# Block-sparse attention and an expert layer: V gathered in 2 KB rows on two queues, weight transfers behind the first V table, the first pairs normalised by VectorE

## The chip, the core and the metric

The kernel runs on one core of a Trainium2 chip. A core has five engines, each with its own in-order instruction queue: TensorE (PE, matmuls and transposes), VectorE (DVE), ScalarE (ACT), GpSimd (POOL) and SyncE (SP, which only issues transfers here). Sixteen DMA engines are shared by the transfers that SP, ACT and POOL issue. Matmuls write to PSUM, eight banks of 2 KB for each of 128 partitions; everything else lives in SBUF or in DRAM. The metric is the device time of one execution in microseconds.

## What is computed

Attention with 4 batches, 8 heads, 768 positions and 64 values per head, on a block mask: positions form 24 blocks of 32, and a query block sees its neighbours, the first and the last block, and three sampled blocks. The first and the last query block see everything. An expert layer with a swish follows.

```
scores = scale * np.matmul(q, k.transpose(0, 1, 3, 2))
mask = np.abs(blk_i - blk_j) <= window
mask = mask | (blk_i == 0) | (blk_j == 0) | (blk_i == n_blocks - 1) | (blk_j == n_blocks - 1)
# sampled_blocks: three more key blocks for each query block
scores = np.where(mask, scores, -1000000000.0)
attn = softmax(scores);  attn_out = np.matmul(attn, v)
x = attn_out.transpose(0, 2, 1, 3).reshape(B * S, H * D)      # 3072 x 512
h = x @ w_in                                                  # 512 x 2048
out = (h * (1.0 / (1.0 + np.exp(-beta * h)))) @ w_out         # 2048 x 512
```

All inputs are float32 (the sampled blocks are integers), and so is the output. Inside, the kernel works in float16 with float32 sums.

## The kernel before

**Attention in pairs.** Query blocks 1 to 22 of each batch form 11 pairs, 44 in all. For a pair n, POOL copies the three sampled key blocks of each of its two query blocks into a tile KG (`kg`, L521, block numbers read into registers), POOL or VectorE copies the neighbours and the first and last block (`kn`), TensorE adds the mask (L600) and the scores (`sc`, L610) into two PSUM banks. VectorE takes the maximum (L621), ScalarE the Exp (L629), VectorE the reciprocal of the sums (L635). The normalising multiply (`nrm`, L641) goes to POOL or VectorE, whichever the plan finds sooner. TensorE transposes the result (`tp`, L653), VectorE copies it out of PSUM (`ptv`, L657), TensorE multiplies it by the gathered V (`av`, L668), and VectorE and ScalarE copy the product into xT (L259, L257).

**V's way.** V is rearranged into Vn (`vperm`, L259 for batch 0), written to a DRAM table VT of 768 rows of 512 float16 values, 1 KB a row (`vtab`: L490 for batch 0 in two halves of the columns, L494 later), and gathered from there into VG, a tile of 128 partitions x 2 query blocks x 2 chunks x 512 values. For each pair SP issues seven transfers (L582): one with the neighbours of both blocks (96 partitions, 192 KB) and six with a sampled block each (32 partitions, 32 KB). The first pair of a batch has two more, with the first and the last block; the next three pairs copy that part from it (`vres`). Four VG tiles take turns. SP first reads a pair's six block numbers into registers (L550).

**The first and the last block** of a batch (`gs`, `gm`, `ge`, `gn`, `gt`, `gav`: L705 to L758) see all keys: four units per batch, each of which holds two banks for its scores.

**The expert layer** works on 96 blocks of 32 tokens in groups of 8, 8, 8, 16, 16, 16, 16 and 8. For a group, TensorE computes 16 row blocks of h (L817, four matmuls each), ScalarE the tanh (L823), VectorE the product g (L828); then TensorE multiplies by w_out (L845), ScalarE scales the result (L263) and issues the output transfer (L863). A group needs the attention output of all its blocks; the first one needs pairs 0 to 3.

**Loads.** SP loads K, Q and V of batch 0 in halves (L388, 768 KB each). POOL loads the weights with a cast to float16, eight transfers for each of w_in and w_out (L417, L423; 64 partitions, 256 KB of float16 each), after a small copy (L403) that waits for V's first half, and after them V, K and Q of batch 1 to 3 (L443).

**The order.** A list scheduler (`Plan.run`) writes the order of all engines once, when the kernel is built. Each task has an engine (or two to choose from), an assumed duration, predecessors, a priority, and PSUM banks to open or close. The scheduler steps through time and gives each free engine the ready task of lowest priority value. `prio` of pair n is 10 n. The transfers are modelled with one shared ring time, and weight transfers wait until the ring is at most 3.2 us ahead (`bulk`). The expert layer may hold four of the eight banks while attention is left. The engines then run that order, and wait with semaphores for what is really late.

Of the kernel before, what the change touches and what calls it, by code (L numbers as in the profile page):

```python
# [22 lines left out]
class Task:  # L23
    def __init__(self, name, eng, dur, emit, deps=(), prio=0.0, lat=0.0,
                 opens=(), closes=(), moe=False, dma=0.0, slack=0.0, hw=0, bulk=None):
        self.on = {eng: dur} if isinstance(eng, str) else dict(eng)
        self.name, self.eng, self.dur, self.emit = name, None, None, emit
        self.deps = [d for d in deps if d is not None]
        self.prio, self.lat = prio, lat
        self.opens, self.closes, self.moe, self.dma = opens, closes, moe, dma  # L30
        self.slack, self.hw, self.bulk = slack, hw, bulk
        self.kind = name.rstrip("0123456789.")
        self.end = None


class Plan:
# [14 lines left out]
    def run(self):  # L51
# [3 lines left out]
        need = {}  # L55
        for t in tasks:
            need[t] = len(t.deps)
# [10 lines left out]
        ring_at = 1.0  # L68
        lanes = [0.0] * 8
# [18 lines left out]
        while done < len(tasks):  # L88
            progress = False
            for e in engines:  # L90
# [3 lines left out]
                for t in waiting[e]:  # L94
# [7 lines left out]
                    if t.bulk is not None and ring_at > now + t.bulk + 1e-9:  # L102
                        continue
# [26 lines left out]
                if t.hw:  # L130
                    at = now
                    for _ in range(t.hw):
                        at = max(at, lanes[issued % 8]) + t.dur / t.hw
                        ring_at = max(ring_at, at + 0.4) + t.dma / t.hw
                        end = lanes[issued % 8] = ring_at + 0.9
                        issued += 1
                    free[e] = at
                elif t.dma:
                    ring_at = max(ring_at, end + 0.6) + t.dma
                    end = ring_at + 1.1  # L140
                t.start, t.end = now, end
                order.append(t)
                heapq.heappush(events, (end, seq, t))
                seq += 1
# [8 lines left out]
            for e in engines:  # L153
                nxt += [ready_at[t] for t in waiting[e] if ready_at[t] > now + 1e-9]
                nxt += [ring_at - t.bulk for t in waiting[e]
                        if t.bulk is not None and ring_at - t.bulk > now + 1e-9]
            nxt += [f for f, _ in bank_free if f > now + 1e-9]
            if not nxt:
                raise RuntimeError("plan is stuck: " + ", ".join(
                    t.name for e in engines for t in waiting[e]))  # L160
            now = max(now, min(nxt))
            while events and events[0][0] <= now + 1e-9:
# [3 lines left out]
                done += 1  # L166
                for s in succ.get(t, ()):
# [15 lines left out]
def kernel(  # L183
# [52 lines left out]
    VG = [sb(f"VG{i}", [P, 2, 2, D_MODEL]) for i in range(NVG)]  # L236
# [13 lines left out]
    plan = Plan(8, 4)  # L250
# [39 lines left out]
    t_sbl = add("sbl", "ACT", 0.5, emit_sbl, prio=-200, dma=0.3, hw=1)  # L290
# [46 lines left out]
    for part, f in enumerate((emit_mask0, emit_mask1, emit_mask2)):  # L337
# [9 lines left out]
    beta_row = osb[0][0:4, :]  # L347
    ident32 = t_sb[1][0:4, 0:8].bitcast(FP32)
    FQ = N_FFC // 4
    t_beta0 = add("beta", "ACT", 0.5, lambda: nc.scalar.dma_start(  # L350
        out=beta_row, in_=moe_beta.rearrange("(q x) -> q x", q=FQ)), prio=-140, dma=0.1, hw=1)
    t_id32 = add("id32", "DVE", 0.2, lambda: nc.vector.tensor_copy(
        out=ident32, in_=identity[0:4, 0:4]), deps=[t_ident], prio=-64)

    def emit_betaT():
        for i in range(4):
            nc.tensor.transpose(out=bank("beta")[:, i * FQ:(i + 1) * FQ],
                                in_=beta_row.rearrange("q (p i) -> q i p", i=4)[:, i, :], identity=ident32)
# [3 lines left out]
        out=beta_sb[:, :].rearrange("x (q i) -> x i q", i=4),  # L362
        in0=bank("beta")[:, 0:N_FFC].rearrange("x (i q) -> x i q", i=4),
# [22 lines left out]
    for i, (nm, t, dst) in enumerate((("K", k, K16), ("Q", q, Q16), ("V", v, None))):  # L386
        for f in range(2):
            tl = add(f"ld{nm}0.{f}", "SP", 0.47, lambda i=i, t=t, f=f: nc.sync.dma_start(  # L388
                out=stage_half(i, f) if i < 2 else v_stage[:, f * HH:(f + 1) * HH, :],
                in_=src6(t, 0, f * HH, HH)), prio=-80 + i * 2 + f, dma=2.0, hw=1)  # L390
# [11 lines left out]
    def touch(dst, src, dep, prio):  # L402
        return add("touch", "POOL", 0.6, lambda: nc.gpsimd.tensor_copy(out=dst, in_=src),  # L403
                   deps=[dep], prio=prio)

    tch = touch(w_in_sb[0:1, 0, 0:1], v_stage[0:1, 0, 0:1], v0ld[0], -58)


    w_in_r = moe_w_in.rearrange("(c p) f -> c p f", p=P)
    w_out_r = moe_w_out.rearrange("(q p i) m -> q p (i m)", p=P, i=4)  # L410
    w_in_v = w_in_sb[:, :, :].rearrange("x c (q p i) -> x c q i p", p=P, i=4)
    t_win, t_wout = [], []
    THR = 3.2
    for c in range(4):
        for f in range(2):
            ps = slice(64 * f, 64 * f + 64)
            t_win.append(add(f"win{c}.{f}", "POOL", 0.85, lambda c=c, ps=ps: nc.gpsimd.dma_start(  # L417
                out=w_in_sb[ps, c, :], in_=w_in_r[c, ps, :]),
                deps=[tch], prio=-50 + 0.2 * c + 0.1 * f, dma=1.3, bulk=THR))
    for c in range(4):  # L420
        for f in range(2):
            ps = slice(64 * f, 64 * f + 64)
            t_wout.append(add(f"wout{c}.{f}", "POOL", 0.85, lambda c=c, ps=ps: nc.gpsimd.dma_start(  # L423
                out=w_out_sb[ps, 4 * c:4 * c + 4, :].rearrange("x i m -> x (i m)"), in_=w_out_r[c, ps, :]),
                deps=[tch], prio=-49 + 0.2 * c + 0.1 * f, dma=1.3, bulk=THR))

# [6 lines left out]
    for b in range(B):  # L433
        pr = prep_prio(b)
        if b:
            vperm[b] = []
            for nm, t, raw, dst in (("V", v, RAW[0], Vn[b % 2]), ("K", k, RAW[1], K16), ("Q", q, RAW[0], Q16)):
                tr = {"K": trK, "Q": trQ}.get(nm)
                for f in range(2):
                    hs = slice(f * HH, (f + 1) * HH)  # L440
                    free = [vperm[b][f]] if nm == "Q" else [perm["QK"["VK".index(nm)], b - 1, f]] if b > 1 else []
                    tl = add(f"ld{nm}{b}.{f}", "POOL", 0.9, lambda t=t, raw=raw, b=b, f=f, hs=hs:
                             nc.gpsimd.dma_start(out=raw[:, hs, :], in_=src6(t, b, f * HH, HH)),  # L443
                             deps=free + [t_wout[-1]] if b == 1 else free,
# [459 lines left out]
```

## Time and profile before

| | |
|---|---|
| median of three runs | 328.34 us (322.41, 328.34, 328.72) |
| the profiled execution | 323.59 us, span 321.8 us |
| mean granted TensorE clock | 0.929 |
| busy: PE, DVE, ACT, POOL | 280.7, 246.7, 216.8, 187.5 us |
| DMA | 43.97 MB in 42211 packets |

The span runs from the first to the last instruction of the profiled execution; what is read from the trace adds up to it. A group line of the profile gives line, engine, operation, output and input tile, shapes and count; then the busy time and the mean of one; then the idle time of the engine just before them and what ended it. The page cuts the span into 40 slices and gives the busy share of each engine in each slice as a digit. The chain of waits follows the work that ended last back to the start. A transfer's time to landing runs from its issue to its completion.

These two groups of the page concern the change directly:

```profile
L668 PE MATMUL bank<-PT,VG 128*128 128x64 f16 x704 | 31.8, 199 | 7.9 <-DMA VG<-VT 5.9
...
L641 POOL TENSOR_SCALAR PP<-PP,ST 128x256 f16<-128x256 f16 x168 | 81.3, 501 | 47.9 <-DVE ST L635 42.4
```

### The profile page before, as it was taken

Reading aid. Unit: us, or ns where it says so; the run is one execution under the profiler, and the core shown is the slowest. Engines: PE = TensorE matmul, PEld = TensorE weight load, DVE = VectorE, ACT = ScalarE, POOL = GpSimd, SP = SyncE. Lnnn points to the kernel's source line nnn. Section 1 sums busy time; section 2 is a strip of 40 time slices with the busy share of each in tenths; the row PEclk is TensorE's granted clock in tenths of the full one; section 3 lists DMA queues with packets and bytes.
Section 4 is the critical chain, followed back from the end, with each engine's and each line's share of the span. In section 5 each row is a group of like instructions: output and inputs, shape, how many; then the busy total and the mean of one; then the engine's idle time right before and its main releaser. Section 6 shows DMA issues by size and latency. Waiting matters only on the chain.

```text
span 321.8 us, 10665 instructions
## 1 busy us (share of the span) xinstructions
PE 280.7 (87%) x3525; PEld 177.3 (55%) x3525; DVE 246.7 (77%) x572; ACT 216.8 (67%) x644; POOL 187.5 (58%) x528
## 2 busy tenths in 40 slices
PE   0845578989979699988979999999999999999994
PEld 0612366956755486556635656555665555554671
DVE  2996579878869989999987667999979975771060
ACT  1676435864968489789687669977679864772361
POOL 2479956848778456798966654756948453200000
PEclk9975557999979989999979999999999999999999
DMA  7889995998697586323777973335232333100201
GB/s 255 332 172 208 229 227 105 187 252 177 132 204 145 164 212 114 107 80 94 125 146 168 226 170 93 88 84 153 94 118 69 91 110 100 33 3 33 98 2 66
DMA packets 42211, 43.97 MB, mean 137 GB/s; under 512 B 6440, under 2 KB 37672, under 8 KB 42156
## 3 DMA queue, kind: packets, MB, share of 16 engines
q1 hardware_dynamic: 27760, 25.71, 27.1%
q0 software_dynamic: 10784, 11.27, 23.4%
q10 hardware_dynamic: 3612, 6.30, 5.4%
q8 instruction: 28, 0.46, 0.6%
q14 instruction: 27, 0.22, 0.2%
HBM read 45.10 MB, written 9.44 MB: 169 GB/s over the span
## 4 chain that ended last, share of the span: by engine, by line
PE 60%; DMA 14%; DVE 12%; ACT 6%; issue 3%; SPq 3%; POOL 1%; POOLq 0%; ACTq 0%; DVEq 0%
PE bank L845 22%; PE bank L817 21%; DMA VG<-VT 6%; PE bank L668 4%; PE bank L653 4%; DMA RAW<-in_k_dram 3%; DMA VT<-Vn 3%; SPq L582 3%; DVE ST L621 2%; ACT PP L629 2%; PE bank L463 2%; DVE g L828 2%; PE bank L610 2%; PE bank L600 2%; DMA sbl<-in_sampled_blocks_dram 1%
## 5 line engine op out<-in xcount | busy, mean ns | idle before, releaser
L641 POOL TENSOR_SCALAR PP<-PP,ST 128x256 f16<-128x256 f16 x168 | 81.3, 501 | 47.9 <-DVE ST L635 42.4
L629 ACT ACTIVATE PP<-bank,ST 128x256 f16<-128x256 f32 x176 | 81.6, 478 | 30.1 <-DVE ST L621 21.5
L817 PE MATMUL bank<-xT,w_in_sb 128*128 128x256 f16 (+1 forms) x512 | 97.1, 338 | 3.9 <-ACT PP L629 1.1
L845 PE MATMUL bank<-w_out_sb,g 128*128 128x512 f16 x384 | 90.9, 380 | 0.0
L828 DVE SCALAR_TENSOR_TENSOR g<-t,bank 128x512 f16<-128x512 f16 (+1 forms) x128 | 66.6, 546 | 22.1 <-ACT t L823 21.3
L823 ACT ACTIVATE t<-bank,beta_sb 128x512 f16<-128x512 f32 (+1 forms) x128 | 69.9, 589 | 14.3 <-PE bank L817 11.6
L817 PEld LDWEIGHTS <-w_in_sb 128*128 128x128 f16 x512 | 55.3, 116 | 30.1 <-issue 8.6
L521 POOL COPY KG<-KT 128x64 f32 x264 | 54.6, 256 | 24.6 <-PE bank L610 17.8
L621 DVE TENSOR_REDUCE ST<-bank 128x2 f32<-128x512 f32 x88 | 57.5, 678 | 7.5 <-PE bank L610 7.4
L845 PEld LDWEIGHTS <-g 128*128 128x128 f16 x384 | 34.7, 98 | 38.6 <-issue 4.1
L668 PE MATMUL bank<-PT,VG 128*128 128x64 f16 x704 | 31.8, 199 | 7.9 <-DMA VG<-VT 5.9
L668 PEld LDWEIGHTS <-VG 128*128 128x128 f16 x704 | 28.3, 102 | 16.5 <-issue 9.6
L629 ACT ACTIVATION_READ_ACCUMULATOR PP<-bank,ST 128x1 f32 x176 | 36.8, 209 | 0.0
L653 PE MATMUL bank<-identity,PP 128*128 128x128 f16 x352 | 30.9, 233 | 6.6 <-ACT xT L257 2.4
L653 PEld LDWEIGHTS <-PP 128*128 128x128 f16 x352 | 24.6, 104 | 15.9 <-issue 4.1
L657 DVE COPY PT<-bank 128x1024 f16<-128x1024 f16 x44 | 30.1, 684 | 4.1 <-PE bank L653 3.3
L259 DVE CAST xT<-bank 64x256 f16<-64x256 f32 (+1 forms) x52 | 20.6, 402 | 12.3 <-PE bank L668 7.5
L263 ACT ACTIVATE osb<-bank 128x512 f32<-128x512 f32 x24 | 14.4, 601 | 20.7 <-PE bank L845 20.7
L257 ACT CAST xT<-bank 64x256 f16<-64x256 f32 (+1 forms) x52 | 17.4, 346 | 15.4 <-DVE xT L259 6.3
L610 PE MATMUL bank<-KG,QT 64*32 64x256 f16 x704 | 20.9, 293 | 1.4 <-POOL KG L521 1.0
L726 ACT ACTIVATE PG<-bank,SG 128x384 f16<-128x384 f32 x32 | 18.4, 583 | 4.9 <-DVE SG L721 4.1
L600 PE MATMUL bank<-maskr,ones 64*32 64x192 f16 (+1 forms) x352 | 14.9, 272 | 5.7 <-ACT PP L629 5.5
(79 smaller groups left out, 256.6 us busy)
## 6 DMA issues: line engine op xcount, KB each, us to landing
VG<-VT SPq DMA_DIRECT2D x268, 32.0 KB, 2.6
VG<-VT SPq DMA_DIRECT2D x40, 192.0 KB, 2.9
out_dram<-osb ACTq DMA_DIRECT2D x20, 256.0 KB, 2.2
RAW<-in_v_dram POOLq DMA_DIRECT2D x6, 384.0 KB, 5.1
RAW<-in_k_dram POOLq DMA_DIRECT2D x6, 384.0 KB, 5.6
VT<-Vn SPq DMA_DIRECT2D x3, 768.0 KB, 6.1
RAW<-in_q_dram POOLq DMA_DIRECT2D x6, 384.0 KB, 6.5
w_in_sb<-in_moe_w_in_dram POOLq DMA_DIRECT2D x8, 256.0 KB, 5.9
```

The costliest lines, as they stand in the source:

```text
L521: nc.gpsimd.tensor_copy(out=kg32[:, g, :, (2 + r) * W:(3 + r) * W], in_=kt32[:, :, bass.ds(vals[3 * g + r], W)])
L610: nc.tensor.matmul(bk[u][hp * BLK:(hp + 1) * BLK, g * 256:(g + 1) * 256], lhsT=QT[b % 2][u * D:(u + 1) * D, hp, (i0 + g) * BLK:(i0 + g + 1 ...
L621: mx[n, u] = add(f"mx{n}.{u}", "DVE", 0.6, lambda n=n, u=u, sb_=sb_: nc.vector.tensor_reduce(out=sb_[:, 0, 2 * u:2 * u + 2], in_=bank(("S" ...
L629: nc.scalar.activation(out=pb[:, u, g, :], in_=bank(("S", n, u))[:, g * 256:(g + 1) * 256], func=AF.Exp, bias=sb_[:, 0, 2 * u + g:2 * u + ...
L641: (nc.vector if eng == "DVE" else nc.gpsimd).tensor_scalar(out=pb[:, u, g, :], in0=pb[:, u, g, :], scalar1=sb_[:, 2, 2 * u + g:2 * u + g + ...
L653: nc.tensor.transpose(out=o[:, s * P:(s + 1) * P], in_=pb[:, u, g, c * P:(c + 1) * P], identity=identity)
L657: ptv[n] = add(f"ptv{n}", "DVE", 0.61, lambda n=n: nc.vector.tensor_copy(out=PT[n % NPT], in_=bank16(("T", n))), deps=[tp[n]] + ([av[n - N ...
L668: nc.tensor.matmul(o[:, (g * NHP + hp) * 64:(g * NHP + hp + 1) * 64], lhsT=vgb[:, g, c, hp * P:(hp + 1) * P], rhs=pt[:, g, c, :, hp * BLK: ...
L817: nc.tensor.matmul(o[:, 0:TW], lhsT=w_in_v[:, c, f // 4, f % 4, :], rhs=xT[:, c, c0:c0 + TW], start=(c == 0), stop=(c == NHP - 1))
L823: lambda G=G, f=f, TW=TW, tt=tt: nc.scalar.activation(out=tt[:, 0:TW], in_=bank(("H", G, f))[:, 0:TW], func=AF.Tanh, bias=0.0, scale=beta_ ...
L828: lambda G=G, f=f, TW=TW, tt=tt, gg=gg: nc.vector.scalar_tensor_tensor(out=gg[:, f, 0:TW], in0=tt[:, 0:TW], scalar=1.0, in1=bank(("H", G, ...
L845: nc.tensor.matmul(o[:, :], lhsT=gg[:, f, s * P:(s + 1) * P], rhs=w_out_sb[:, f, :], start=(f == 0), stop=(f == N_FFC - 1))
```

## The change

- **2 KB rows.** A VG tile becomes 128 partitions x 2 x 1024 values: a partition holds two neighbouring rows of V. A sampled block fills 16 partitions, the neighbours 48, and each packet's row is 2 KB. So that the two chunks match, the transposes of the probabilities take the even and then the odd columns.
- **Two queues.** For pairs 0 to 3, ScalarE reads the block numbers of the second query block and issues its three gathers; SP keeps the rest. Later pairs are issued by SP alone.
- **The first V table** is one transfer after both halves of Vn, and its copies come ahead of the casts in priority. The small copy on POOL (L403) goes.
- **Eight weight transfers** of 512 KB: w_in by two row blocks and half the columns, w_out by two row groups. The first waits for the K gather of pair 1, the other seven for the V table to land. The first half of h needs the first two, the other half the other two; each quarter of the second product needs one of w_out. Batch 1's loads come behind the last weight transfer in the order, without waiting for it to land.
- **Normalising** of pairs 0 to 3 always goes to VectorE.
- **The first and last block** of batch 0 wait for the scores of pair 4 (two units) and pair 5.
- **The scheduler** gets a model with three rings that share the DMA engines, eight lanes for the transfers of SP and ACT, other durations in places, and five banks for the expert layer instead of four. Beta is transposed in two steps instead of four.

The core of the diff:

```
+class Rings:
+    START = {"SP": 0.4, "ACT": 0.4, "POOL": 1.0}
+    LAND = {"SP": 0.9, "ACT": 0.9, "POOL": 2.0}
...
-    VG = [sb(f"VG{i}", [P, 2, 2, D_MODEL]) for i in range(NVG)]
+    VG = [sb(f"VG{i}", [P, 2, 2 * D_MODEL]) for i in range(NVG)]
-    plan = Plan(8, 4)
+    plan = Plan(8, 5)
...
-    tch = touch(w_in_sb[0:1, 0, 0:1], v_stage[0:1, 0, 0:1], v0ld[0], -58)
-    w_in_v = w_in_sb[:, :, :].rearrange("x c (q p i) -> x c q i p", p=P, i=4)
+    NI = 2
+    NACT, NDVE, GFIRST = 4, 4, 4
+    w_out_r = moe_w_out.rearrange("(q p i) m -> p q (i m)", p=P, i=NI)
+    w_in_v = w_in_sb[:, :, :].rearrange("x c (q p i) -> x c q i p", p=P, i=NI)
+    THR, SLACK = 3.2, 4.0
+    w_in_r = moe_w_in.rearrange("(c p) f -> p c f", p=P)
+    for f in range(2):
+        fs = slice(f * D_FF // 2, (f + 1) * D_FF // 2)
+        for c in range(0, NHP, 2):
+            t_win.append(add(f"win{f}.{c}", "POOL", 0.7, lambda c=c, fs=fs: nc.gpsimd.dma_start(
+                out=w_in_sb[:, c:c + 2, fs], in_=w_in_r[:, c:c + 2, fs]), ...
+    for c in range(0, N_FFC // NI, 2):
+        t_wout.append(add(f"wout{c}", "POOL", 0.7, lambda c=c: nc.gpsimd.dma_start(
+            out=w_out_sb[:, NI * c:NI * c + 2 * NI, :].rearrange("x (q i) m -> x q (i m)", i=NI),
+            in_=w_out_r[:, c:c + 2, :]), ...
...
-                    deps=[v0ld[f]], prio=-65))
-                vtab[0].append(add(f"vtab0.{f}", "SP", 0.45, ... out=vt_rows[:, :, cs], in_=Vn[0][:, :, cs] ...
+                    deps=[v0ld[f]], prio=-73))
+            vtab[0].append(add("vtab0", "SP", 0.45, lambda vt_rows=vt_rows: nc.sync.dma_start(
+                out=vt_rows, in_=Vn[0]), deps=vperm[0], prio=-64, dma=(8, 0.234)))
+            for t in t_win[1:] + t_wout:
+                t.deps += vtab[0]
...
-                    bass.AP(tensor=vt.tensor, offset=vt.offset + (i0 - 1) * BLK * D_MODEL,
-                            ap=[[D_MODEL, 3 * BLK], [BLK * D_MODEL, 2], [1, D_MODEL]]))
+                    vgb[5 * HB:P, :, :],
+                    bass.AP(tensor=vt.tensor, offset=vt.offset + (i0 - 1) * BLK * D_MODEL,
+                            ap=[[W2, 3 * HB], [BLK * D_MODEL, 2], [1, W2]]))
             for g in range(2):
-                for r, (c, s) in enumerate(((0, 2), (0, 3), (1, 0))):
-                    yield 0.1, lambda v, g=g, r=r, c=c, s=s: (
-                        vgb[s * BLK:(s + 1) * BLK, g, c, :], vt[bass.ds(v[3 * g + r], BLK), :])
+                for r in range(3):
+                    yield g, 1, lambda v, g=g, r=r: (
+                        vgb[(2 + r) * HB:(3 + r) * HB, g, :], two(vt[bass.ds(v[r], BLK), :]))
+            act = g == 1 and on_act
+                (nc.scalar if act else nc.sync).dma_start(out=o, in_=i)
...
-                copy_on(eng, vgb[0:2 * BLK, :, 0, :], h64.to_broadcast([2 * BLK, 2, D_MODEL]))
+                copy_on(eng, vgb[0:BLK, :, :], src[0:BLK, 0:1, :].to_broadcast([BLK, 2, 2 * D_MODEL]))
...
-        nrm[n] = add(f"nrm{n}", {"POOL": 1.85, "DVE": 0.8}, None, emit_nrm, deps=[rc], prio=pr - 0.5)
+        nrm[n] = add(f"nrm{n}", {"DVE": 0.87} if n < NDVE else {"POOL": 2.2 if n < 8 else 1.85, "DVE": 0.85}, ...
-                                            in_=pb[:, u, g, c * P:(c + 1) * P], identity=identity)
+                                            in_=pk[:, u, g, c, :], identity=identity)
...
+                         [evQ[b, hp] for hp in range(NHP)] + ([sc[GFIRST + w // 2]] if b == 0 else []), ...
+    t_win[0].deps.append(kg[1])
```

## The prediction

> **What bounds the kernel now.** I read the page's slices first, then the chain of waits, then the opening by itself.
>
> In the slices (8 us each) a digit is the busy share in tenths, and PEclk the granted TensorE clock:
>
> ```profile
> PE   0845578989979699988979999999999999999994
> PEclk9975557999979989999979999999999999999999
> DMA  7889995998697586323777973335232333100201
> ```
>
> From slice 21 on TensorE is full to the end. It is empty in slice 0 and half empty in slices 2 to 5 (16 to 48 us), at half clock there, while the DMA engines are full. So work is lost in the opening. The busy times of the stretches (length in us, then PE, PEld, DVE, ACT, POOL, clock, DMA share, GB/s) say how much:
>
> ```profile
> 16.00:54.00 38.00, 22.97 (x367) 14.53 (x351) 30.18 (x80) 20.48 (x81) 30.27 (x85) 0.60 0.89 189
> 54.00:165.00 111.00, 99.40 (x1420) 70.18 (x1420) 99.00 (x234) 84.75 (x265) 82.46 (x221) 0.95 0.72 156
> 165.00:281.00 116.00, 115.62 (x1476) 66.61 (x1475) 93.91 (x198) 87.46 (x258) 69.28 (x203) 0.99 0.44 113
> ```
>
> TensorE idles 15 us in the first, 11.6 us in the second, 0.4 us in the third. After 281 us there are only expert-layer matmuls, back to back. Every microsecond by which that layer's first matmul (L817, at 53.7 us) moves forward is therefore worth up to one at the end, as far as the work it needs is not merely pushed behind it.
>
> What holds it is in the chain of waits (start, length, what):
>
> ```profile
> 17.85 8.90 DMA VT<-Vn
> ...
> 30.33 6.78 DMA VG<-VT
> 37.49 7.29 DMA VG<-VT
> ...
> 53.83 3.32 PE bank L817 x16
> ```
>
> V is written to the DRAM table, read back as gathered blocks, and only then can pairs 0 to 3 be multiplied; group 0 of the expert layer needs all four. The DMA view of 16 to 50 us (queue: packets, MB, share of 16 engines) shows who fills the engines:
>
> ```profile
> q0 software_dynamic: 1280, 4.20, 67.6%
> q1 hardware_dynamic: 3752, 2.53, 25.6%
> ```
>
> q0 carries the weights: 0.676 x 34 us = 23.0 us of all sixteen engines, running against the V table and the gathers (q1, 8.7 us). A 32 KB gather took 5.2 us to land in this stretch, against 2.6 us in 90 to 160 us.
>
> **The change, part by part.**
>
> *V table.* Today its halves leave at 15.74 and 17.85 us and both land 8.9 us later; last at 26.75. The two Vn copies (0.99 and 0.94 us, L259) have KG copies ahead of and between them (14.06 to 14.80, 15.72 to 16.96). V's loads were issued at 3.3 and 4.0 us and landed 10.2 to 11.4 us later, so by 15.4. Ranked first, the copies run from 14.1 to 16.0–16.4 and the KG copies take their place: VectorE's sum up to 17.75 us is the same. One DMA of 768 KB leaves at about 16.4. Its landing: 3.3 us (the same table in 90 to 160 us) to 8.9 us (in 54 to 90 us, among loads). Only one weight transfer runs beside it; I take 5.5 us. It lands at **22** (19.7 to 25.3).
>
> *Gathers.* Pairs 0 to 3 need 9 + 3 x 7 = 30. SP put them out from 26.80 to 47.87: 0.70 us each, of which 0.42 is issue and the rest waits for earlier gathers (5.1 us in nine waits) and registers. ScalarE takes 12, SP keeps 18: 7.6 us at 0.42, 12.6 at 0.70, then 2.6 us to land. Pair 3 has V between 32 and 38; I take **36**. The packets: q1 as a whole took 27.1% of 16 x 321.8 us for 27760, so 50 ns for one of 0.93 KB; the 2 KB output rows of q10 took 5.4%, so 77 ns each. A 2 KB packet in place of two saves 23 ns: some 12 us of the sixteen engines over the kernel, which wait for nothing after 165 us; there I count zero.
>
> *Weights.* Eight transfers of 512 KB instead of sixteen of 256 KB. One leaves after pair 1's K gather, seven after the V table: 7/8 x 23.0 = 20.1 us of DMA, plus 4.0 us of gathers (1664 KB, 52 packets of 77 ns for each engine), from 22, and the landing: last one at 47 to 50 us (47.7 today), the four of w_in at 35 to 40. The first group's second matmuls (L845) need the last only after 64 matmuls of the first layer, so this is covered. POOL issued sixteen in 9.2 us; eight with 256 rows cost between 0.53 (64 rows) and 0.78 us (the RAW loads' 512) each, about 5.2. The touch (0.31) goes.
>
> *Normalising on VectorE.* Today pair 0 took 0.87 us on DVE, pairs 1 to 3 took 1.85 to 2.02 on POOL (L641), whose queue was full from 24 to 40 us and delayed them. Now +2.6 us for DVE, -5.9 for POOL.
>
> *VectorE as the next limit.* From 17.75: four pairs' maxima 5.1, reciprocals 0.7, normalising 3.5, PT copies 2.8, half the xT casts 1.7, three shared-block copies 1.9, KG copies 1.1, and pairs 4 and 5's maxima between, 2.6: 19.4, so **37.2**. It and the gathers end together. With the last product, casts and hops (2.3 us), L817 starts at **39.5** instead of 53.7: 14.2 us earlier.
>
> *What is pushed behind.* The global rows of batch 0 (L705 to L747) now wait for pair 4. Before 53.7 they cost DVE 7.6 us (maxima 4.6, sums 0.9, normalising 0.4, PTG copies 1.6), TensorE 4.2 us at half clock, 2.1 at full. If DVE binds what follows, 14.2 - 7.6 = 6.6 us are left; if TensorE, 12.1. Between 54 and 165 us both are busy 99 of 111 us, so I take the middle, 9.3.
>
> *Small edits.* The shared-block copy goes from 64 x 1024 (0.41 DVE, 1.04 POOL) to 32 x 2048: between the same and double. Nine times after the opening: 0 to 3.7 us of DVE, part of it idle; I take 1.0. Transposes (L653) now read every second column. Nearest row: L745 reads every sixth, its weight loads take 125 ns against 98, but six in the chain take 0.34 us, 57 ns each, against 0.45 for eight of L653: zero, and up to 352 x 27 ns = 9.5 us if they ever ceased to be hidden. w_in's step goes from four to two: its 113 ns loads lie under 216 ns matmuls: zero. Beta: two transposes fewer, hidden behind DVE. The loads of batch 1 lose their wait for the last weight (V1 left at 51.95, K1 at 60.4, landing at 71.6, where DVE waited 1.8 us); with the gather waits of 54 to 165 us (1.9) I count 0.7 of these 3.7 as won.
>
> **Sum:** 9.3 - 1.0 + 0.7 = 9.0 us. The profiled execution took 323.6 us (span 321.8), so **314.6 us**. The three runs shown have a median of 328.3 and a lowest of 322.4; the profiled one lies near the lowest, and my number is for such an execution. A repeat can differ by some 2%, which is also about what a measurement tells from no change.
>
> The rest of the order is unknown: a list scheduler rewrites it with other durations, and the expert layer may hold five of eight banks instead of four. Its bounds are the 11.6 us of TensorE idling in 54 to 165 us: half of it won or lost.
>
> **Rivals.**
>
> *ScalarE becomes the bound.* Its twelve gathers and four register loads (0.74 for six values on SP, so 0.37) cost 6.5 to 9.9 us at 0.42 to 0.70 each, in order, before later Exps. In 16 to 39 us it was busy 13.2 of 23 us, so the issue fits, the waits may not. If 6 of the 9 us are lost to late Exps of pairs 3 to 7: 320.6. Chance 0.18.
>
> *Narrow gathers are slow.* A random block now lands in 16 partitions instead of 32. If its packets took four times the 77 ns, the opening's 24 random gathers cost 24 x 0.23 = 5.6 us more while the engines are full: 320.2. Against it: 32 KB in 32 partitions land in 1.6 us at best, 192 KB in 96 have a median of 2.9, so size hardly shows. Chance 0.07. The Trainium skill speaks for this one ("SBUF — State Buffer", Door 1: The DMA port swizzle): bandwidth follows how many of the sixteen ports the partitions reach, and 16 partitions reach four where 32 reach eight. No run here shows it.
>
> *The table lands late, and three queues stand behind it: slower.* Today SP alone waits for it (8.4 us). Now ScalarE waits before its first gather and POOL before its second weight transfer, with the Exps of pairs 1 to 3 and the K gathers of pairs 2 and 3 behind them in order. Each microsecond of landing after 22 costs one. With 7.6 us pushed behind, the gain of 6.6 is gone when it lands at 28.6; at 33 to 36, if the first weight transfer's packets go ahead of it on every engine, the time is 328 to 331. For it: today's 8.9 us beside weights. Against: one transfer, not four, runs beside it. Chance 0.13.
>
> *The order also fills 54 to 165 us.* Half of 11.6 us more: 308.8. Chance 0.10.
>
> My forecast (310 to 319) keeps 0.52. Faster than 317.1: nearly all of it and the last case, 0.60; slower than 330.1: most of the third, 0.11; between, 0.29. The range 306 to 327 leaves out some 0.06 below and 0.12 above.
>
> **What would show it.** The table's landing near 22 in the chain; pair 0's product (L668) near 27 instead of 34.5 to 37; L817's first matmul near 40; PE digits of 6 to 8 in slices 3 to 5 and the half clock ending before 45 us; gathers landing in about 3.5 us in the opening. Wrong if ScalarE's waits on DMA show several microseconds, if L817 starts after 46, or if TensorE's idling in 54 to 165 us grows by what the opening gained.

## The result and the profile after

The changed kernel takes 344.84 us (median of four, 342.26 to 347.25) against 325.38 us (320.94 to 328.72) for the kernel before, measured beside it: 1.072 times as long, interval 1.0555 to 1.0883. It is slower by some 19 us, where 9 us faster was forecast. The profiled execution took 342.26 us, span 340.2, at a mean clock of 0.978 (before 323.59, 321.8 and 0.929), so the clock is not what costs.

The slices of the page, of the changed kernel (8.5 us each here, busy share in tenths):

```profile
PE   1753549986697889975999989994999997999995
PEclk9999999997999999995999999998999999999999
DMA  7779999899233999326656295213322314400101
```

The half clock of the opening is gone, and it brought nothing: TensorE is no fuller than before in slices 2 to 5, and has new gaps in slices 9, 10, 18 and 27. The busy times of the three stretches (us of the stretch, then PE, PEld, DVE, ACT, POOL, clock, DMA share, GB/s) of the changed kernel:

```profile
16.00:54.00 38.00, 20.73 (x377) 13.71 (x377) 26.68 (x65) 18.93 (x76) 27.67 (x90) 1.00 0.91 183
54.00:165.00 111.00, 91.23 (x1256) 61.88 (x1255) 86.20 (x207) 77.66 (x237) 72.31 (x190) 0.95 0.69 149
165.00:281.00 116.00, 109.45 (x1443) 62.60 (x1442) 98.42 (x218) 86.03 (x265) 75.25 (x212) 0.99 0.42 104
```

TensorE idles 17.3, 19.8 and 6.6 us in them, where it idled 15.0, 11.6 and 0.4. The last two, 14.4 us more together, hold most of the 18.4 us by which the span grew, and TensorE's work is the same (281.4 us for 280.7). So the loss lies in the steady part, which the prediction had counted as nearly untouched.

What ends the idling, in the page's groups of the changed kernel (busy us, mean ns, then the idle time before and its releasers):

```profile
L708 POOL TENSOR_SCALAR PP<-PP,ST 128x256 f16<-128x256 f16 x160 | 76.9, 497 | 41.7 <-DVE ST L702 41.4
...
L736 PE MATMUL bank<-PT,VG 128*128 128x64 f16 x704 | 31.4, 199 | 30.1 <-DMA VG<-VT 26.1
```

The P V products waited 26.1 us for gathered V, against 5.9. Normalising hardly moved off POOL (160 of 176 multiplies, 168 before). And why V came late, from the waits of SP's queue (us in total, times, longest), of the kernel before and then of the changed one:

```profile
SPq L582 <- DMA VG<-VT: 9.0, 14, 1.4
SPq L582 <- DMA out_dram<-osb: 8.1, 4, 4.2
```

```profile
SPq L650 <- DMA out_dram<-osb: 54.5, 15, 7.6
...
SPq L650 <- DMA VG<-VT: 16.5, 16, 2.4
```

SP, which issues the gathers, stood 54.5 us waiting for output transfers, which ScalarE issues and with which a gather shares no data. The chain of waits from 68 to 94 us of the changed kernel (start, length, what) shows such a wait end to end, twice:

```profile
70.23 3.51 DMA out_dram<-osb
...
73.75 0.32 SPq L650
...
74.76 5.03 DMA VG<-VT
...
79.87 0.60 PE bank L736 x8
...
80.56 7.67 DMA out_dram<-osb
...
88.25 2.54 DMA VG<-VT
```

An output leaves at 70.23 and lands at 73.74; the next gather leaves at 73.75 and the second behind it at 74.76. That one lands at 79.78, and the products start at 79.87, after TensorE has stood idle for 3.45 us. The following output leaves at 80.56, takes 7.67 us, and a gather leaves 0.02 us after it has landed.

**How a gather comes to wait for an output.** In the built kernel the transfers of SP and ScalarE take eight semaphores in turn, in one common order, and each waits until the transfer eight places ahead of it has landed. The common order is not the one of the kernel's own scheduler: the layer that records the program merges the two queues into it. I compared the built programs of the changed kernel and of one with 1 KB rows (below). SP's sequence is the same in both, and so is ScalarE's; the merged order is not. Number of gathers that stand ahead of each of the first twelve outputs:

```
kernel before, 1 KB rows    65  72 103 110 140 153 153 199 205 206 213 252
changed, with 1 KB rows     72  77  97 110 139 148 150 192 202 207 216 259
changed, 2 KB rows          62  74  87  97 132 140 140 186 192 193 203 234
kernel before, 2 KB rows    52  65  93 102 130 140 141 185 195 203 205 231
```

With 2 KB rows an output of the changed kernel stands some ten gathers (3 to 25), about one and a half pairs, further ahead; that many fewer can SP issue before an output has landed. The four traces give the same numbers: each transfer of SP and ScalarE carries its semaphore there, and eight of them take turns, 45 or 46 times each. By that order the 70th gather of the changed kernel waits for the first output and the 81st for the second. The trace agrees: 69 gathers had left by 73.74 us, when the first output landed, and 80 by 88.23. That the recording layer moves the outputs because it takes narrow transfers for slower is my guess; I only saw that it moves them.

### The profile page after: what moved, and what is told of

Read it like the earlier page. It is cut to its first block, busy times and chain, and to the rows that moved or that the text cites. A ratio compares the mean times of both kernels' runs of the same rounds, so it can differ in the third digit from the quotient of the medians.

```text
span 340.2 us, 10662 instructions
## 1 busy us (share of the span) xinstructions
PE 281.4 (83%) x3523; PEld 171.9 (51%) x3523; DVE 245.5 (72%) x566; ACT 217.4 (64%) x647; POOL 187.4 (55%) x522
## 3 DMA queue, kind: packets, MB, share of 16 engines
q1 hardware_dynamic: 17248, 25.32, 24.8%
q0 software_dynamic: 11680, 11.27, 23.1%
## 4 chain that ended last, share of the span: by engine, by line
PE 44%; DMA 22%; DVE 16%; ACT 6%; SPq 5%; issue 4%; POOL 1%; POOLq 1%; ACTq 0%; DVEq 0%
PE bank L915 16%; PE bank L887 15%; DMA VG<-VT 15%; SPq L650 5%; DMA out_dram<-osb 4%; PE bank L736 3%; PE bank L721 3%; DVE g L898 3%; DVE ST L688 3%; ACT PP L696 2%; PE bank L516 2%; DVE SG L787 2%; DMA VT<-Vn 1%; DMA g<-in_k_dram 1%; DVE PT L725 1%
## 5 line engine op out<-in xcount | busy, mean ns | idle before, releaser
L708 POOL TENSOR_SCALAR PP<-PP,ST 128x256 f16<-128x256 f16 x160 | 76.9, 497 | 41.7 <-DVE ST L702 41.4
L887 PE MATMUL bank<-xT,w_in_sb 128*128 128x256 f16 (+1 forms) x512 | 95.6, 335 | 1.5 <-ACT PP L696 0.9
L915 PE MATMUL bank<-w_out_sb,g 128*128 128x512 f16 x384 | 92.9, 382 | 0.2 <-ACT PG L794 0.2
L887 PEld LDWEIGHTS <-w_in_sb 128*128 128x128 f16 x512 | 48.9, 100 | 33.1 <-issue 6.6
L736 PE MATMUL bank<-PT,VG 128*128 128x64 f16 x704 | 31.4, 199 | 30.1 <-DMA VG<-VT 26.1
L311 ACT CAST xT<-bank 64x256 f16<-64x256 f32 (+1 forms) x56 | 19.3, 352 | 41.1 <-PE bank L736 22.3
L313 DVE CAST xT<-bank 64x256 f16<-64x256 f32 (+1 forms) x48 | 18.7, 398 | 32.0 <-ACT xT L311 18.7
L317 ACT ACTIVATE osb<-bank 128x512 f32<-128x512 f32 x24 | 14.4, 601 | 19.8 <-PE bank L915 19.7
L805 POOL TENSOR_SCALAR PG<-PG,SG 128x768 f16<-128x768 f16 x15 | 14.7, 979 | 21.0 <-DVE SG L802 10.7
L677 PE MATMUL bank<-KG,QT 64*32 64x256 f16 x704 | 21.2, 304 | 3.8 <-POOL KG L313 2.0
L313 POOL COPY KG<-KT 128x384 f32<-128x384 f32 (+3 forms) x46 | 22.0, 497 | 0.0
```

The source lines that it names most:

```text
L313: (nc.vector if eng == "DVE" else nc.gpsimd).tensor_copy(out=out, in_=in_)
L708: (nc.vector if eng == "DVE" else nc.gpsimd).tensor_scalar(out=pb[:, u, g, :], in0=pb[:, u, g, :], scalar1=sb_[:, 2, 2 * u + g:2 * u + g + ...
L736: nc.tensor.matmul(o[:, (g * NHP + hp) * 64:(g * NHP + hp + 1) * 64], lhsT=vgb[:, g, c * D_MODEL + hp * P:c * D_MODEL + (hp + 1) * P], rhs ...
L887: nc.tensor.matmul(o[:, 0:TW], lhsT=w_in_v[:, c, f // NI, f % NI, :], rhs=xT[:, c, c0:c0 + TW], start=(c == 0), stop=(c == NHP - 1))
L915: nc.tensor.matmul(o[:, :], lhsT=gg[:, f, s * P:(s + 1) * P], rhs=w_out_sb[:, f, :], start=(f == 0), stop=(f == N_FFC - 1))
```

## The experiments

The expectations of the first four runs name three theories: **O**, gathers wait for outputs through the shared semaphores; **G**, the opening and the new order were simply overrated; **L**, in the opening it does not matter who issues a gather. From the fifth run on, **P** (place) is theory O with its cause, the place of the outputs among the gathers, against **W** (width), by which transfers into 16 partitions are slow by themselves. A result is given as the median, with the lowest and the highest run, and then as the ratio to the kernel before with its 95% interval. The kernel before took 326.36, 326.62, 327.2 and 324.91 us (medians) beside the four sets of runs: the first four runs, the next four (up to the outputs from POOL with 2 KB rows), the next three, and the last one alone. So a difference of some 2 us between runs of two sets is not told from none.

### Leaving the outputs out

Both kernels without 22 of the 24 output steps, so most results stay on the chip:

```
             def emit_od(...):
+                if k < 22:
+                    return
```

> The changed kernel with its written order kept, without 22 of the 24 output transfers (they are left out; only the last two tiles are written). Theory O: the loss is that SP's gathers take one of eight transfer semaphores in turn with ScalarE's output transfers, so that a gather waits until an output issued eight transfers earlier in the written order has landed (54.5 us of SP's waits). Then SP's waits on outputs vanish, TensorE's waits on gathers after 60 us fall from 16 to below 6 us, and the time falls by 12 to 18 us, to 324 to 331. Theory G: the loss comes from the opening, from gathers and weights that land later than the order supposes; the outputs only wait in the meantime. Then at most 4 us are gained, 338 or more.

> The kernel before with its written order kept, without the same 22 output transfers (left out), as the control: SP waited 8.1 us in four waits for outputs there, and TensorE 2 us for gathers after 60 us. Theory O: 0 to 4 us gained, 317 to 322. Theory G says nothing else here; a gain above 8 us would mean that output traffic itself costs time and would weaken O.

The changed kernel took 319.89 us (319.08 to 324.64), 0.982 times the complete kernel before (0.9798 to 0.9842). The kernel before took 322.34 us (319.91 to 323.88), 0.9866 (0.9793 to 0.9938). So the outputs cost the changed kernel 25 us, more than the 12 to 18 expected, and the one before 4 us, and without them the changed one is the faster by 2.5 us. The outputs' data are no answer: both kernels write the same. This bears theory O out; G explains at most what is missing from the forecast gain. That the order of the outputs is what matters, and not their writing as such beside narrower gathers, this run can't tell; the runs below do.

### All gathers from SP

```
-                (nc.scalar if act else nc.sync).dma_start(out=o, in_=i)
+                nc.sync.dma_start(out=o, in_=i)
```

> The changed kernel with its written order kept, but the twelve gathers of ScalarE issued by SP at the same places. Theory L: the opening's gathers go at eight in flight over 5 to 6.5 us of landing, 0.7 us each whoever issues them. Then the products of pairs 0 to 3 move by less than 2 us and the total stays within 3 us of the changed kernel. Rival, the step of the prediction: SP's issuing is the limit. Then pair 3's product comes 4 us later or more and the total is 3 us or more longer.

346.02 us (345.44 to 346.59), 1.0617 (1.0571 to 1.0663): within some 1 us of the changed kernel, and pair 3's products started at 48.99 us for 49.66. The second issuing queue was worth nothing, and its waits were not the loss either, which ends the rival "ScalarE becomes the bound".

### 1 KB rows, all else of the change kept

The VG tile, the gathers, the shared-block copy and the transposes' columns go back to the form of the kernel before; each engine's order is the changed kernel's.

```
-    VG = [sb(f"VG{i}", [P, 2, 2 * D_MODEL]) for i in range(NVG)]
+    VG = [sb(f"VG{i}", [P, 2, 2, D_MODEL]) for i in range(NVG)]
```

> The changed kernel with its written order kept, but V gathered in 1 KB rows into 32 partitions as before, and the plain column order in the transposes. If 2 KB packets help (23 ns less per KB pair), the opening's gathers land 0.5 to 1.5 us later and the total grows by 0 to 3 us. If narrow gathers into 16 partitions are slow, landing shortens and the total falls by 3 us or more. If the 2 KB rows do not matter here, within 2 us.

323.19 us (322.38 to 324.83), 0.9908 (0.9877 to 0.9939). I had expected at most 3 us and got 21.7: the rows, which I had priced at zero, carry the whole loss, and without them the rest of the change is a gain of about 3 us. This is also the version that beats both kernels. Its waits of SP and of TensorE (us, times, longest):

```profile
SPq L650 <- DMA VG<-VT: 21.1, 19, 5.6
...
SPq L650 <- DMA out_dram<-osb: 4.7, 2, 3.0
```

```profile
PE bank L736 <- DMA VG<-VT: 5.6, 5, 2.4
```

4.7 us for outputs instead of 54.5, with the same outputs at much the same times (the first at 70.57 for 70.23 us).

### Place or width: the two taken apart

Two kernels cross rows and order. One keeps the 2 KB rows and makes each output that stands elsewhere wait also for the gather behind which it stands with 1 KB rows, so that the recording layer has to put it there (the trace has the first six behind gather 73, 77, 99, 111, 140 and 151). The other keeps the 1 KB rows and gives 19 gathers the very waits for outputs that they have in the changed kernel.

```
+        for a_, b_ in PLACE:     # (output, gather) pairs or (gather, output) pairs
+            tc.add_manual_dep(x, y.name, how, reason="place")
```

> The changed kernel with its 2 KB rows, each of the outputs made to wait for one earlier gather, so that in the order in which SP's and ACT's transfers take the eight semaphores it stands where it stands in the kernel with 1 KB rows (behind gather 72, 77, 97, 110, 139, 148, ... instead of 62, 74, 87, 97, 132, 140, ...). Each engine's own order is kept. Theory P (place): the rows cost nothing by themselves; they only put the outputs ahead of gathers that SP would issue early, and the eighth transfer behind an output waits for it. 320 to 328 us, SP's waits for outputs from 54.5 us to under 15, PE's for VG from 26.1 to under 10. Theory W (width): a transfer into 16 partitions is slow and makes the outputs land late whatever the order: 337 to 347 us, waits for VG of PE at 20 us or more.

> The other corner: 1 KB rows into 32 partitions, and 19 gathers made to wait for the output that the gather of the same number waits for in the changed kernel (gather 69 for output 0, 80 for 1, 94 for 2, 104 for 3, 138 for 4, ...). Theory P: these waits are the loss, 335 to 346 us, SP's waits for outputs at 35 us or more. Theory W: 321 to 326 us, like 1 KB rows without them (323.19).

| | outputs late in the order | outputs early, 15 waits or more |
|---|---|---|
| 1 KB rows | 323.19 us | **343.67 us** (342.42 to 346.72), 1.0629 (1.0469 to 1.079) |
| 2 KB rows | **332.53 us** (332.14 to 333.28), 1.0258 (1.0141 to 1.0374) | 344.84 us |

SP's waits with 1 KB rows and the added waits, and then with 2 KB rows and the outputs moved back:

```profile
SPq L651 <- DMA out_dram<-osb: 57.9, 15, 7.2
```

```profile
SPq L651 <- DMA out_dram<-osb: 12.0, 3, 6.5
```

The waits alone make the loss: gathers into 32 partitions with them are as slow as gathers into 16 (343.67 against 344.84). In the other direction 12.3 of 21.7 us came back, fewer than expected, and TensorE's waits for V fell to 15.1 us and not to under 10; 11.6 of these lie ahead of 60 us. The order was moved by real waits of the outputs for gathers, and ScalarE's queue shows a price for that, beside the few waits for outputs that are left. With the outputs moved back:

```profile
ACT xT L311 <- DMA VG<-VT: 12.4, 2, 7.0
```

It was 7.6 us in one wait with 1 KB rows. The second wait here, 5.4 us, is the added one, in the timeline of ScalarE:

```profile
72.01 0.59 ACT L317 ACTIVATE osb<-bank 128x512 f32<-128x512 f32 x1
77.53 0.38 ACTq L934 DMA_DIRECT2D out_dram<-osb  x1
```

The first output's data stood ready at 72.60 us, but the transfer left at 77.53, when the gather that it was made to wait for had landed, and ScalarE stood still meanwhile; the 65th product with w_in starts at 81.6 us, and at 74.9 with 1 KB rows. So part of the missing 9.3 us is the price of this way of moving the outputs. How they divide between it, the three waits for outputs that are left and the width of the gathers this pair can't tell; the next runs bound the width.

### The rows alone, on the kernel before

The VG tile, the gathers, the shared-block copy and the transposes' columns take the new form in the kernel before; all its gathers stay on SP, in its own order.

```
-    VG = [sb(f"VG{i}", [P, 2, 2, D_MODEL]) for i in range(NVG)]
+    VG = [sb(f"VG{i}", [P, 2, 2 * D_MODEL]) for i in range(NVG)]
```

> The kernel before with the 2 KB rows alone, its order kept, all gathers on SP, normalisation and weights as they were. The outputs move here too (behind gather 63, 77, 106 of the transfers' order instead of 76, 84, 116). Theories P and W alike: 335 to 348 us, that is the rows carry the whole loss without the rest of the change. If the loss needs the new opening or the second issuer, 322 to 329 us.

346.1 us (343.32 to 347.51), 1.0703 (1.0577 to 1.0828), and SP's waits:

```profile
SPq L587 <- DMA out_dram<-osb: 43.9, 13, 7.3
```

(The places 63, 77, 106 and 76, 84, 116 of the expectation count all transfers that stand ahead, the table above gathers alone.) Neither the second issuer, nor the weights, nor the new order of the opening is needed for the loss.

### Outputs that take none of the eight semaphores

POOL issues the outputs, at the same places of the program; its transfers have semaphores of their own. This was done with 2 KB and with 1 KB rows, and beside it the 1 KB rows ran without outputs, by the first experiment's edit.

```
-                    nc.scalar.dma_start(out=out[base + row:base + row + P, :], in_=ob)
+                    nc.gpsimd.dma_start(out=out[base + row:base + row + P, :], in_=ob)
```

> The changed kernel with 2 KB rows, its 28 output transfers issued by POOL, so that they take none of the eight semaphores that SP and ACT share; the places in the order are kept. Theory P: no gather waits for an output, 317 to 326 us. Theory W: the gathers themselves land no sooner, PE's waits for VG stay above 20 us and the time above 335. Should POOL's issue hold up its gathers of K and the normalisations, POOL shows waits for osb and the time stays above 330 with few waits for VG.

> 1 KB rows with the outputs issued by POOL, orders kept: the partner of the changed kernel with POOL's outputs (329.0 us). The two differ in the rows alone, and no gather of either waits for an output's semaphore. Place alone: 326 to 332 us, the same within 3 us, and no better than 1 KB rows with ACT's outputs by more than 2 (POOL waited 36 us for osb there). Width has a price of its own: 317 to 324 us, 5 or more below the partner. It is also the candidate for a version faster than both kernels, at 320 or less.

> 1 KB rows, 22 of the 24 output steps left out (the results stay on the chip), orders kept: the partner of the changed kernel without outputs (319.89 us). Place alone: 318 to 321 us, the rows make no difference once no output stands among the gathers. Width: 312 to 316 us.

With 2 KB rows 329.0 us (325.2 to 332.15), 1.0095 (1.0024 to 1.0166); with 1 KB rows 325.11 us (323.46 to 326.54). Most of the loss is gone with the shared semaphores, though less than expected: POOL now stands in the outputs' place.

```profile
POOL out_dram L933 <- ACT osb L317: 36.2, 6, 15.9
```

That is the view of waits with 2 KB rows. It is no better way than 1 KB rows alone. The 1 KB partner came between my two cases, 3.9 us below (3.5 without the two longest of the ten runs with 2 KB rows), and TensorE's waits for V were 10.8 us there and 18.5 with 2 KB rows. So the width probably has a small price of its own, and the run with 2 KB rows missed the 317 to 326 us expected of place alone. Without outputs (22 of 24 left out, as above) 1 KB rows take 318.37 us (317.91 to 321.73), 0.9737 (0.9631 to 0.9844), against 319.89 with 2 KB rows. So where no gather waits for an output, the width costs 1.5 us in one pair and 3.9 us in the other: at most a fifth of the loss, and 1.5 us is within the spread of the runs and of the sets.

### What spaces the gathers of the opening

This leaves one question: why the first product with w_in, forecast for 39.5 us, came at 52.23, and even with 1 KB rows at 52.54. The chain of the changed kernel from 17 to 53 us:

```profile
17.91 4.74 DMA VT<-Vn
...
22.67 4.13 DMA VG<-VT
...
28.24 7.53 DMA VG<-VT
...
35.78 6.63 DMA VG<-VT
...
42.43 5.27 DMA VG<-VT
...
49.67 1.00 PE bank L736 x16
...
52.30 0.76 PE bank L887 x3
```

The table landed at 22.65 us, where it was expected. From there landings of gathers follow each other, four of 4.1 to 7.5 us and from 47.72 us on a last one of 1.95. The moment one has landed, the gather eight places behind it leaves: at 35.77 and 35.78 us, and at 42.41 and 42.43. The eight weight transfers were cut to an eighth of their bytes, 16 of 128 rows; the rest of both weights is zero, so the second part computes with mostly zeros. VectorE fills in the zeros first, which delays its first work.

```
-                out=w_in_sb[:, c:c + 2, fs], in_=w_in_r[:, c:c + 2, fs]),
+                out=w_in_sb[0:16, c:c + 2, fs], in_=w_in_r[0:16, c:c + 2, fs]),
```

> The changed kernel with 2 KB rows, and its eight weight transfers cut to an eighth of their bytes (16 of 128 rows; the rest of both weights is zero, filled by VectorE ahead of its first work, which may move the opening back by up to 3 us). This leaves out most of what the second part computes with, not the work itself. It asks what spaces the first 30 gathers 0.7 us apart and has pair 3's P V products start at 49.7 and the first product with w_in at 52.2. If the 16 DMA engines' throughput does (they are busy all the time between 20 and 40 us, over half of it with weights): the gathers come at 0.45 us or less, pair 3 starts at 40 to 45 and the first product at 42 to 48 us. If the latency of a transfer with eight in flight does, whatever the traffic: 0.6 us or more, and 50 to 53. The whole time should stay above 335 us, since the later waits for outputs stay; below 330 would mean that the opening carries the loss after all.

> 1 KB rows, and the eight weight transfers cut to an eighth of their bytes as in the changed kernel's run (16 of 128 rows, the rest zero and filled by VectorE, which issued the first V table 4 us later there): the second part's products are computed with mostly zero weights. With 2 KB rows the first product with w_in came 6.3 us sooner (45.9 for 52.2 us) and the end did not move (343.04). Theory P: the end stayed because the waits of the gathers for outputs set the pace behind the opening; with 1 KB rows, where there are few of them, the opening counts: the first product at 45 to 48 for 52.5 us, and 315 to 319 us for 323.19. If the opening counts for nothing here either, that is if what is gained is given back to later stages in any case: 321 to 325 us, and then the sum of the prediction was wrong in kind and not in size.

The chain of the changed kernel with an eighth of the weights, 21 to 48 us:

```profile
21.88 4.98 DMA VT<-Vn
...
27.26 2.85 DMA VG<-VT
...
30.13 3.34 DMA VG<-VT
...
33.56 1.03 PE bank L736 x16
...
38.65 1.77 DVE ST L688 x3
```

The views of 22 to 43 us of ScalarE's twelve gathers (KB each, median us to landing), and the stretch of 20 to 40 us (as above), first of the changed kernel, then with an eighth of the weights:

```profile
VG<-VT ACTq DMA_DIRECT2D x12, 32.0 KB, 5.5
...
20.00:40.00 20.00, 9.56 (x195) 5.88 (x195) 15.77 (x40) 9.50 (x40) 15.78 (x57) 1.00 1.02 198
```

```profile
VG<-VT ACTq DMA_DIRECT2D x12, 32.0 KB, 2.9
...
20.00:40.00 20.00, 12.43 (x264) 7.70 (x264) 19.00 (x47) 11.71 (x49) 18.86 (x69) 1.00 0.54 138
```

SP's 32 KB gathers landed in 3.2 us with an eighth of the weights, for 6.4. The first 30 leave in 12.8 us instead of 21.2, 0.44 us each instead of 0.73, and behind the first pair VectorE, ScalarE and TensorE make the chain, no gather. The first product with w_in starts at 45.89 us, though the table left 4.0 us later: 24.0 us behind the table's issue instead of 34.3. So it is the traffic: with full weights the DMA engines are busy all the time from 20 to 40 us (share 1.02), with an eighth 0.54. It acts through the landing: with eight transfers in flight, 5.5 to 6.4 us of landing make 0.69 to 0.80 us a gather, and 2.9 to 3.2 us make 0.36 to 0.40 (an estimate from these rows, against 0.73 and 0.44 measured).

That gain of 6.3 us did not reach the end: 343.04 us (342.22 to 343.85), 1.0455 (1.0328 to 1.0582), and SP waited 61.4 us for outputs. With 1 KB rows the first product came at 48.28 instead of 52.54 us, and the time was 318.41 us (317.81 to 319.28), 0.986 (0.9766 to 0.9954), instead of 323.19. These 4.8 us are between two sets, and the ratios (0.986 for 0.9908) are not clear of each other. The traces bear them out: with 1 KB rows the first product with w_in starts 4.3 us sooner and the last one 6.9 (304.4 for 311.3 us); with 2 KB rows the 6.3 us are 2.7 at the 193rd product (139.5 for 142.2) and gone at the last (330.6 for 328.9). So with 2 KB rows the waits of the gathers for the outputs set the pace behind the opening, and what is gained ahead of them is waited away.

## Why the prediction was wrong

The forecast was 314.6 us, the profiled execution took 342.3. Of the 27.7 us between, some 21.7 are the rows (344.84 less 323.19 us), and the other 6 or so are what the rest of the change fell short by, 3 us gained for 9.0 forecast. The opening would account for these: the first product with w_in moved by 1.5 us and not by 14.2. That share is argued; no run measures it by itself.

**Gathers, the packets' term: the step that failed.** "A 2 KB packet in place of two saves 23 ns: some 12 us of the sixteen engines over the kernel, which wait for nothing after 165 us; there I count zero." The packets did go (17248 of them on q1 for 27760), but they saved 1.5 us of the sixteen engines and not 12: q1 and q10 together took 30.3% of 340.2 us, 103.1, for 32.5% of 321.8, 104.6. That size hardly matters. What failed is the zero, the rows priced as if they could act on the engines' time alone: a gather also waits for whatever holds its semaphore, and with the rows the outputs took other places. In place of zero the runs showed 54.5 us of SP's waits for outputs and 21.7 us of the time. The view of SP's waits on the kernel before had the row, 8.1 us for outputs in four waits. I had no term for it, and did not ask what places those four.

**Gathers, the opening's term: mis-sized.** "ScalarE takes 12, SP keeps 18: 7.6 us at 0.42, 12.6 at 0.70, then 2.6 us to land." Two queues do not halve what the DMA engines and eight semaphores limit together; the pace stayed at 0.73 us for one. The 2.6 us were the landing in a stretch without weights; in the stretch at hand it was 5.5 to 6.4 us, and 5.2 us was what I had read there in the kernel before. The Trainium skill says that spreading transfers over engines saves only the time to issue them, since all run on the same sixteen DMA engines ("DMA: Bandwidth & Descriptors", "Issuing engines are not separate DMA queues"). The run with SP alone agrees: 346.02 us for 344.84.

**VectorE as the next limit: borne out, where it could show.** With an eighth of the weights the first product came 24.0 us behind the table's issue; my sum said 23.1 (39.5 less 16.4), and VectorE was busy 19.0 of the 20 us from 20 to 40. It had also started 4 us late there, behind the zeros, so the near agreement is in part luck. With the weights beside the gathers it never became the limit.

**V table: right, with some luck.** 22 forecast (19.7 to 25.3), landing at 22.65. It left 1.5 us later than forecast and took 4.74 us instead of 5.5, two errors that partly cancel.

**Weights: w_in right, w_out late.** The last of w_in landed at 39.6 us, within the 35 to 40 I gave. The last of w_out was issued at 54.2 and landed at 59.9, for 47 to 50. TensorE's first product with w_out starts at 63.5, so it is not on the chain. But in ordering seven of them behind the table I saw only what they gain it, and not that they then run beside the gathers, 58.8% of the engines' time in 16 to 56 us.

**Normalising, small edits, batch 1's loads.** POOL kept 160 of 176 multiplies, as planned. The loads left later than before (V1 at 61.2 us for 51.95), not earlier, so the 0.7 us counted for them was not there. The transposes with a step of two cost nothing that can be seen (their weight loads' median is 98 ns in both kernels).

**The rivals.** "Narrow gathers are slow" named the right edit, the rows, with 0.07 and at 320 us, and by the wrong mechanism. The Trainium skill's rule behind it ("SBUF — State Buffer", Door 1: The DMA port swizzle), by which 16 partitions reach half the ports of 32, is borne out by 1.5 and 3.9 us at most; from 150 to 300 us a 32 KB gather landed in 2.0 us with 16 partitions and 2.3 with 32. The rival on the slower side, a late table with three queues behind it, did not happen. Of the signs of being wrong two showed: the first product with w_in started at 52.23 us, past 46, and TensorE's idling in 54 to 165 us grew by 8.2 us, more than the 1.5 that the opening gained. The signs of being right that concern the gathers failed too: pair 0's product came at 33.94 us instead of 27, and a gather landed in 5.5 us or more instead of 3.5. None of the signs looked at SP's waits for outputs.

**Left open.** How the 9.3 us by which 332.53 stays above 323.19 divide, what the width costs by itself (1.5 and 3.9 us by the two pairs, near the spread), and why the recording layer places them as it does.

## What to carry to other kernels

Where two queues share a few semaphores in turn, a transfer waits for one that has nothing to do with it: look in the waits of the issuing queue for tiles that the instruction does not touch, and look again after any change of a transfer's shape, since the merged order can move though no queue's own order does. A landing time belongs to the stretch that it was read in, and more issuing queues do not help where the DMA engines are full. A gain in the opening counts at the end only if nothing behind it sets its own pace: test that by taking the suspected traffic away with and without the later waits.

## What the runs showed that I had not expected

The full clock in the opening (1.00 from 16 to 54 us for 0.60) is worth nothing there, since TensorE waits for data (17.3 us idle for 15.0). Unrelated transfers coupled by eight semaphores cost some 20 us of 344 in 15 waits, the longest 7.6 us. And cutting seven eighths of the weights' bytes out of the opening halved a gather's landing, from 5.5 to 6.4 us to 2.9 to 3.2.
